# In the late turns of a fused attention and MLP kernel, sums of values and chunk 4's scores become one group on TensorE

## The chip, the cores and the metric

The kernel runs on one core of one Trainium2 chip. The metric is device time in microseconds (us) of one execution. A core has TensorE (PE in the profile; its weight loads are PEld), VectorE (DVE), ScalarE (ACT), GpSimd (POOL) and SyncE (SP), which here issues transfers. Each engine runs its own instructions in the order in which they stand in its queue, and waits on semaphores for the others.

## The reference

Inputs are q, k, v (8 batches, 8 heads, 576 positions, 64 dimensions), w_in (512 x 2048) and w_out (2048 x 512), all float32.

```python
scores = scale * np.matmul(q, k.transpose(0, 1, 3, 2))
mask = block_i >= block_j                 # blocks of 64 positions
scores = np.where(mask, scores, -1000000000.0)
scores = scores - np.max(scores, axis=-1, keepdims=True)
attn = np.exp(scores)
attn = attn / (np.sum(attn, axis=-1, keepdims=True) + 1e-09)
attn_out = np.matmul(attn, v)
...
x = attn_out.transpose(0, 2, 1, 3).reshape(4608, 512)
h = x @ w_in
g = h * (1.0 / (1.0 + np.exp(-1.702 * h)))
out = g @ w_out
```

## The kernel before

Attention goes by *turns*: turn n handles pair n, two heads of one batch, 32 turns in all, four to a batch. The 576 queries of a pair are five *chunks*: chunk 0 has 64 queries, chunks 1 to 4 have 128 each, and chunk i sees the first 64 × (2i+1) keys. The experts (the MLP) go by 12 *tiles* of 384 tokens, and each tile by 16 *expert chunks*: 12 products into `hp` (the first matrix, with x and w_in each split in a high and a low part, `xh`, `xl`, `wih`, `wil`), then tanh on ACT, the gate `g` on DVE, its split `gh` (ACT) and `gl` (POOL), and 9 products into `acc` one expert chunk later.

Both are woven into one stream on TensorE. `ORDER` and its special rows set, in 13 slots of a turn, where attention stands: `3+0/2+1` are the scores of chunks 3, 0, 2, 1; `4` those of chunk 4; `V` the sums of values of the pair before (`av`); `L` the preparation of the next pair (`prep`: DVE transposes q and k into `qk`, then SP loads the pair after that into `raw`). Between the slots `advance` emits expert work by a clock of estimated times. From turn 8 on (*late* turns) a slot's attention work is emitted behind the 12 hp products of an expert chunk, so that on TensorE it stands between `hp` and `acc`. TensorE's products keep the order of the program; the queues of the other engines are ordered by Tile's scheduler, by priorities, and gates and splits have a raised one.

PSUM has eight banks: three for `acc`, three turning ones (`w0` to `w2`, from `bank()`) and two (`h`, `w3`) between which `hp` alternates in late turns. A group may borrow the one that hp does not use (`lent_bank`); then the next hp product takes the same bank as the last, and waits for its gate.

A score chunk goes like this: TensorE writes scores of each head into a bank, DVE reads them (`weigh`, mask, scale and minimum in one, line 366), ACT takes exp (line 373), DVE normalises the sums (383, 386), POOL (chunks 0 to 3) or DVE (chunk 4) scales by them, and in late turns DVE transposes blocks into `turned` (`turn`, lines 400 and 405). Behind chunk 4, SP issues 16 copies within `turned` (line 412) that complete the transposition. The next turn's `av` reads them: 60 instructions, 30 products of float32 in two passes, 1600 columns for a head, the two heads side by side; ACT copies the sums into `xr`, a ring of two batches. At a tile's start `split` casts `xr` to `xh` on ACT and subtracts to `xl` on DVE, in four parts, one for each 128 of the model's dimensions; `xh` and `xl` exist once, so a part is overwritten when the last hp products of the tile before have read it. The four pairs of a batch fill one of the four parts each.

Of the kernel before, what the change touches and what calls it, by code (L numbers as in the profile page):

```python
# [25 lines left out]
ORDER = (  # L26
# [3 lines left out]
)  # L30

START = "1+0 - B 2/3 L C - V - 4 - a - - -"
FIRST_LATE = "3+0/2+1 - - - - - V - 4 - - L -"
HANDOVER = "B C - 3+0/2+1 - - V - - - 4 - - L - -"


WEIGHTS_BY = ((0, 0), (8, 13), (14.5, 32))
# [4 lines left out]
def attention_moe_kernel(  # L42
# [21 lines left out]
    NPAIR = B * H // 2  # L64
    HP = H // 2
    NCH = 5

    sp = ctx.enter_context(tc.tile_pool(name="sp", bufs=1))
    d2 = ctx.enter_context(tc.tile_pool(name="d2", bufs=2))
# [5 lines left out]
    def early(n):  # L75

        return n < 2 * HP
# [6 lines left out]

    turns = {"n": 0, "bank": 0, "experts": False, "late": False}
    gate_bank = {"now": "h", "spare": "w3", "lent": False}
    conv = {"step": 0, "loaded": 0}

# [7 lines left out]
    def lent_bank():  # L98
        gate_bank["lent"] = True
        return ps.tile([P, 512], F32, tag=gate_bank["spare"], name="bank")  # L100

    def next_hp():
        if turns["late"] and not gate_bank["lent"]:
            gate_bank["now"], gate_bank["spare"] = gate_bank["spare"], gate_bank["now"]
        gate_bank["lent"] = False
        return ps.tile([P, 512], F32, tag=gate_bank["now"], name="hp")

    def mm(**kw):
        return tc.keep_in_program_order(nc.tensor.matmul(**kw))  # L109
# [205 lines left out]
    def score(n, banks):  # L315

        turns["late"] = not early(n)
        if n not in stats:
            mx = d2.tile([P, NCH + 1, 2], F32, tag="mx", name="mx")
            sm = d2.tile([P, NCH, 2], F32, tag="sm", name="sm")  # L320
            stats[n] = (mx, sm)
        todo = []
        taken = 0
        for chunks in banks:

            part = []
            for lo, hi in ((0, 512),) if width(chunks[0]) <= 512 else ((0, 256), (256, S)):
                ss = []
                for _ in range(2):
                    taken += 1  # L330
                    ss.append(lent_bank() if taken == 1 and turns["late"] else bank())
                c = 0
                for i in chunks:
                    a, z = qrange(i)
                    w = min(hi, width(i)) - lo
                    for hd in range(2):
                        r = slice(hd * D, hd * D + D)

                        mm(
                            out=ss[hd][:, c : c + w], lhsT=qk[n][r, 0, a : a + P],  # L340
                            rhs=qk[n][r, 1, lo : lo + w], start=True, stop=True,
                        )
                        part.append((i, hd, lo, lo + w, ss[hd][0 : z - a, c : c + w]))
                    c += w
            todo.append(sorted(part, key=lambda x: (chunks[::-1].index(x[0]), x[2])))
        for chunks, part in zip(banks, todo):
            e = {}
            for i, hd, lo, hi, s in part:
                e[i] = weigh(n, i, hd, lo, hi, s, e.get(i))
            for i in chunks[::-1]:  # L350
                normalise(n, i, e[i])
                if not early(n):
                    turn(n, i, e[i])

    def weigh(n, i, hd, lo, hi, s, e):
        mx, sm = stats[n]
        a, z = qrange(i)
        m = z - a
        w = width(i)
        if early(n):  # L360
            e = es[i]
        elif e is None:
            e = d2.tile([P, 2, w], F32, tag=f"e{i % 2}", name="e", bufs=1)
        last = i > 0 and hi == w
        mk = mask[0:m, MW - (hi - lo) : MW] if last else mask[0:m, 0 : hi - lo]
        nc.vector.tensor_tensor_reduce(  # L366
            out=e[0:m, hd, lo:hi], in0=s, in1=mk,
            op0=ALU.add, op1=ALU.min, scale=-0.125,
            scalar=3e38 if lo == 0 else mx[0:m, NCH, hd : hd + 1],
            accum_out=mx[0:m, i, hd : hd + 1] if hi == w else mx[0:m, NCH, hd : hd + 1],  # L370
        )
        if hi == w:
            nc.scalar.activation(  # L373
                out=e[0:m, hd], in_=e[0:m, hd], func=AF.Exp, scale=-1.0,
                bias=mx[0:m, i, hd : hd + 1], accum_out=sm[0:m, i, hd : hd + 1],
            )
        return e

    def normalise(n, i, e):
        _, sm = stats[n]  # L380
        m = BLK if i == 0 else P
        c = sm[0:m, i]
        nc.vector.tensor_scalar(
            out=c, in0=c, scalar1=1e-9, scalar2=2.0, op0=ALU.add, op1=ALU.mult
        )
        nc.vector.reciprocal(out=c, in_=c)
        on = SCALE_ON[phase(n)][i]
        for hd in range(2):
            x, sc = e[0:m, hd], c[:, hd : hd + 1]
            if on == "P":  # L390
                nc.gpsimd.tensor_tensor(out=x, in0=x, in1=sc.to_broadcast([m, width(i)]), op=ALU.mult)  # L391
            elif on == "D":
                nc.vector.tensor_scalar(out=x, in0=x, scalar1=sc, scalar2=None, op0=ALU.mult)
            else:
                nc.scalar.activation(out=x, in_=x, func=AF.Copy, scale=sc)
# [48 lines left out]
    def av(n):  # L444

        b, h = divmod(n, HP)
        before_av(n)
        o = bank()
        o0 = lent_bank() if turns["late"] else bank()

        todo = []
        for i in range(1, NCH):
            c = (i - 1) * P
            todo += [(o, c, P, j, pw[:, :, SLOT[i] + j]) for j in range(i)]
            todo.append((o, c + BLK, BLK, i, pw[:, 2:4, 9 + i]))
        last = len(todo) - 1
        todo.append((o0, 0, BLK, 0, pw[:, 0:2, 10]))

        for x, (bk, c, nn, j, w) in enumerate(todo):
            for hd in range(2):  # L460
                mm(
                    out=bk[hd * D : hd * D + D, c : c + nn].rearrange("d (a c) -> d a c", c=32),
                    lhsT=values(n)[:, hd, j], rhs=w[:, :, hd], start=x in (0, last + 1), stop=x >= last,
                )
        c0 = (b % 2) * S
        nc.scalar.copy(out=xr[:, h, c0 : c0 + BLK], in_=o0[:, 0:BLK])
        nc.scalar.copy(out=xr[:, h, c0 + BLK : c0 + S], in_=o)
        m = follower(n)
        if m is not None:
            load_v(m)  # L470

    def follower(n):

# [1 line left out]
        return None if m is None or m >= NPAIR else m  # L475

    def order(n):
        return {HP: START, 2 * HP: HANDOVER, 2 * HP + 1: FIRST_LATE}.get(n, ORDER[phase(n)]).split()

    def step(n):  # L480

# [43 lines left out]
    def moe():  # L525
# [24 lines left out]
        for t in range(NT):  # L550
# [6 lines left out]
            for fc in range(NFC):  # L557
                if t == 0:
                    convert(fc // FG * GROUP + NDC + fc % FG + 1)
                hp = next_hp()  # L560
                fs = slice(fc % FG * P, (fc % FG + 1) * P)
                terms = [(wa, xb, dc) for dc in range(NDC) for wa, xb in (("wih", xh), ("wil", xh), ("wih", xl))]
                if fc == 0:

                    terms.sort(key=lambda x: x[1] is xl)
                for cnt, (wa, xb, dc) in enumerate(terms):
                    mm(
                        out=hp[:, 0:tt], lhsT=weights(wa, fc // FG)[:, dc, fs], rhs=xb[:, dc, 0:tt],
                        start=cnt == 0, stop=cnt == 3 * NDC - 1,
                    )  # L570
                    if cnt % 3 == 2:
                        yield unit1(tt)
                g = d2.tile([P, TT], F32, tag="g", name="g", bufs=1)[:, 0:tt]
                gh = d2.tile([P, TT], F32R, tag="gh", name="gh")[:, 0:tt]
                gl = d2.tile([P, TT], F32R, tag="gl", name="gl")[:, 0:tt]

                with tc.high_priority(offset=300):
                    nc.scalar.activation(out=g, in_=hp[:, 0:tt], func=AF.Tanh, scale=1.702)  # L578
                    nc.vector.scalar_tensor_tensor(  # L579
                        out=g, in0=g, scalar=1.0, in1=hp[:, 0:tt], op0=ALU.add, op1=ALU.mult  # L580
                    )

                if fc == NFC - 1 and t + 1 < NT:
                    yield ("tile", t + 1)
                    split(t + 1)
                with tc.high_priority(offset=300):
                    nc.scalar.copy(out=gh, in_=g)  # L587
                    subtract(nc.gpsimd, gl, g, f(gh))
                yield ("gate", fc)
                if prev is not None:  # L590
                    yield from second(prev)
                prev = (gh, gl, fc, acc, t)
# [88 lines left out]
```

## Time and profile before

| | us |
|---|---|
| median of 3 runs | 1104.87 (1103.06 to 1105.16) |
| the profiled execution | 1105.26 |
| its span from first to last instruction | 1103.5 |
| TensorE busy | 1068.6 (97%) |
| DVE, ACT, POOL busy | 584.8, 498.2, 406.5 |

Matmuls are pipelined, and their ends in the profile are modelled: the distance from one start to the next tells more than a duration. In the timeline "x60" is a run of equal instructions shown as one row. What stands in brackets is idle time of the engine ahead of the row, and what ended it. The late turns lie between 186 and 953 us; behind them come experts alone.

### The profile page before, as it was taken

The page shows a single profiled execution, that of the slowest core. Times are in us where ns is not written, and L with a number is a line of the kernel's source. Part 1 is how long each engine was busy: PE and PEld are TensorE (multiplying, and loading weights), DVE is VectorE, ACT ScalarE, POOL GpSimd, SP SyncE. Part 2 cuts the span into 40 slices and gives each one's busy share as a digit, 9 for nine tenths or more (in the row PEclk, how much of TensorE's full clock was granted, in tenths as well). Part 3 has the DMA queues.
Part 4 walks back from the last instruction along what each step waited for, and adds up shares of the span by engine and source line. Part 5 has one row for each costly group of instructions (what it writes and reads, how often), then busy time and mean ns, then how long its engine had stood idle before and what let it go on. Part 6 is the DMA issues. An engine that isn't in the chain of part 4 may idle for free.

```text
span 1103.5 us, 19999 instructions
## 1 busy us (share of the span) xinstructions
PE 1068.6 (97%) x6960; PEld 914.1 (83%) x6960; DVE 584.8 (53%) x1856; ACT 498.2 (45%) x1321; POOL 406.5 (37%) x509
## 2 busy tenths in 40 slices
PE   5869999999999999999999999999999999999998
PEld 3757777788888888888888888888888888899997
DVE  6786786655654655655555555554654655111211
ACT  5865775544443533533534444443443443232322
POOL 4665565333333333323333333333333323222222
PEclk8979999999999999999999999999999999999999
DMA  8734523343334433243444333244443331200000
GB/s 175 206 90 155 147 62 81 71 107 71 93 75 87 115 76 78 62 99 67 109 87 86 89 85 71 59 104 86 87 107 74 74 89 40 55 29 1 30 1 29
DMA packets 219365, 91.25 MB, mean 83 GB/s; under 512 B 197760, under 2 KB 197760, under 8 KB 219264
## 3 DMA queue, kind: packets, MB, share of 16 engines
q1 hardware_dynamic: 214528, 89.38, 34.5%
q10 hardware_dynamic: 4736, 0.59, 0.3%
q8 instruction: 55, 0.90, 0.3%
q14 instruction: 46, 0.38, 0.1%
HBM read 45.09 MB, written 9.44 MB: 49 GB/s over the span
## 4 chain that ended last, share of the span: by engine, by line
PE 87%; DVE 4%; ACT 4%; issue 1%; SPq 1%; DMA 1%; POOL 0%; POOLq 0%; DVEq 0%; ACTq 0%
PE hp L109 35%; PE acc L109 35%; PE bank L109 16%; ACT turned L373 1%; SPq L412 1%; PE bank L112 1%; DVE wm L244 1%; ACT wm L229 1%; DVE wm L233 1%; DVE turned L366 1%; DVE wm L239 1%; DMA raw<-in_k_dram 0%; DVE qk L307 0%; DVE xl L83 0%; ACT turned L426 0%
## 5 line engine op out<-in xcount | busy, mean ns | idle before, releaser
L83 POOL TENSOR_TENSOR gl<-g,gh 128x384 fp32r<-128x384 f32 x192 | 194.5, 1013 | 543.3 <-ACT gh L587 428.8
L579 DVE SCALAR_TENSOR_TENSOR g<-g,hp 128x384 f32<-128x384 f32 x192 | 106.0, 552 | 313.6 <-ACT g L578 312.3
L109 PE MATMUL hp<-xh,wih 128*128 128x384 f32 x768 | 261.1, 340 | 4.2 <-DVE g L579 3.5
L109 PE MATMUL hp<-xh,wil 128*128 128x384 f32 x768 | 258.7, 337 | 0.0
L109 PE MATMUL hp<-xl,wih 128*128 128x384 f32 x768 | 254.8, 339 | 0.2
L578 ACT ACTIVATE g<-hp 128x384 f32<-128x384 f32 x192 | 94.2, 490 | 354.5 <-PE hp L109 352.5
L109 PE MATMUL acc<-woh,gh 128*128 128x512 f32 x576 | 233.9, 406 | 0.0
L109 PE MATMUL acc<-wol,gh 128*128 128x512 f32 x576 | 227.0, 394 | 0.0
L587 ACT CAST gh<-g 128x384 fp32r<-128x384 f32 x192 | 98.4, 513 | 158.7 <-DVE g L579 158.5
L109 PE MATMUL acc<-woh,gl 128*128 128x512 f32 x576 | 168.0, 393 | 0.3 <-POOL gl L83 0.3
L109 PEld LDWEIGHTS hp<-xh,wih 128*128 128x128 f32 x768 | 144.6, 188 | 17.1 <-DVE g L579 4.5
L109 PEld LDWEIGHTS hp<-xh,wil 128*128 128x128 f32 x768 | 144.5, 188 | 7.6
L373 ACT ACTIVATE e<-e,mx 64x64 f32<-64x64 f32 (+4 forms) x240 | 132.2, 552 | 33.0 <-DVE mx L366 33.0
L391 POOL TENSOR_TENSOR e<-e,sm 64x64 f32<-64x64 f32 (+1 forms) x192 | 113.6, 612 | 86.2 <-ACT e L373 43.9
L109 PEld LDWEIGHTS hp<-xl,wih 128*128 128x128 f32 x768 | 144.0, 188 | 1.0 <-DVE xl L83 1.0
L109 PEld LDWEIGHTS acc<-woh,gh 128*128 128x128 f32 x576 | 108.2, 188 | 34.2 <-issue 10.3
L109 PE MATMUL bank<-qk 64*128 64x320 f32 (+4 forms) x768 | 121.3, 428 | 13.5 <-DVE qk L307 10.9
L109 PEld LDWEIGHTS acc<-woh,gl 128*128 128x128 f32 x576 | 107.6, 188 | 25.4 <-POOL gl L83 1.2
L366 DVE CUSTOM_DVE_ANT_0 e<-bank,mask 64x64 f32<-64x64 f32 (+4 forms) x240 | 89.7, 417 | 63.9 <-PE bank L109 60.5
L109 PEld LDWEIGHTS acc<-wol,gh 128*128 128x128 f32 x576 | 108.4, 188 | 16.8 <-issue 0.4
L400 DVE STREAM_TRANSPOSE turned<-e 128x384 f32<-128x384 f32 (+1 forms) x192 | 92.5, 500 | 49.0 <-POOL e L391 48.6
L109 PEld LDWEIGHTS bank<-qk 64*128 64x128 f32 x768 | 69.8, 194 | 52.7 <-issue 22.4
(50 smaller groups left out, 958.8 us busy)
## 6 DMA issues: line engine op xcount, KB each, us to landing
turned<-turned SPq DMA_DIRECT2D x192, 80.0 KB, 2.1
turned<-turned SPq DMA_DIRECT2D x96, 112.0 KB, 2.2
raw<-in_q_dram SPq DMA_DIRECT2D x128, 72.0 KB, 2.3
out_dram<-osb SPq DMA_DIRECT2D x36, 256.0 KB, 2.4
raw<-in_k_dram SPq DMA_DIRECT2D x120, 72.0 KB, 2.4
turned<-turned SPq DMA_DIRECT2D x96, 88.0 KB, 2.1
words<-in_moe_w_in_dram SPq DMA_DIRECT2D x16, 512.0 KB, 6.0
vp<-in_v_dram SPq DMA_DIRECT2D x60, 128.0 KB, 2.5
```

The lines of the kernel that those rows point to most:

```text
L83: eng.tensor_tensor(out=out, in0=in0, in1=in1, op=ALU.subtract)
L109: return tc.keep_in_program_order(nc.tensor.matmul(**kw))
L112: return tc.keep_in_program_order(nc.tensor.transpose(**kw))
L229: nc.scalar.activation(out=bits[j][:, c], in_=f(w[..., 1]), func=AF.Copy, scale=2.0**-112)
L233: nc.vector.tensor_scalar(out=u, in0=u, scalar1=3, scalar2=None, op0=ALU.logical_shift_left)
L366: nc.vector.tensor_tensor_reduce(out=e[0:m, hd, lo:hi], in0=s, in1=mk, op0=ALU.add, op1=ALU.min, scale=-0.125, scalar=3e38 if lo == 0 else ...
L373: nc.scalar.activation(out=e[0:m, hd], in_=e[0:m, hd], func=AF.Exp, scale=-1.0, bias=mx[0:m, i, hd : hd + 1], accum_out=sm[0:m, i, hd : hd ...
L391: nc.gpsimd.tensor_tensor(out=x, in0=x, in1=sc.to_broadcast([m, width(i)]), op=ALU.mult)
L400: nc.vector.transpose(out=tw[:, :, SLOT[i] : SLOT[i] + i, hd].rearrange("p b j c -> p j b c"), in_=e[:, hd, 0 : i * P],)
L578: nc.scalar.activation(out=g, in_=hp[:, 0:tt], func=AF.Tanh, scale=1.702)
L579: nc.vector.scalar_tensor_tensor(out=g, in0=g, scalar=1.0, in1=hp[:, 0:tt], op0=ALU.add, op1=ALU.mult)
L587: nc.scalar.copy(out=gh, in_=g)
```

## The change

`V` and `4` of a late turn become one group. In turn n `av(n - 1)` first sums the values of pair n − 1 into two turning banks: `o0` takes queries 0 to 319, `o` takes 320 to 575. Behind them it writes pair n's scores of chunk 4: for both heads the first 384 keys into two banks of their own (the borrowed one and the third turning one), and the last 192 keys into the free columns of `o0` and `o`. ACT copies the sums out, and `settle` does the rest of chunk 4, with `prep(n + 1)` behind its reads in place of slot `L`. The group stands in slot 8, where chunk 4's scores stood; the sums of values come from slot 5. The scores of the other chunks stay in slot 1. A new dependency (`behind`) puts the third gate after them behind the last read of scores on DVE.

```diff
-    "3+0/2+1 - - - V - - 4 - - - L -",
+    "3+0/2+1 - - - - - - V - - - - -",
...
-FIRST_LATE = "3+0/2+1 - - - - - V - 4 - - L -"
-HANDOVER = "B C - 3+0/2+1 - - V - - - 4 - - L - -"
+HANDOVER = "B C - 3+0/2+1 - - - - - - V - - - - -"
...
+    def behind(ins, other):
+        tc.add_manual_dep(
+            ins.ins, other.ins.name, mybir.DependencyInfo(mybir.DependencyClass.NoSync, mybir.DependencyReason.DATA),
+            reason="order on one engine",
+        )
...
+    def settle(n, banks, todo):
         for chunks, part in zip(banks, todo):
             e = {}
             for i, hd, lo, hi, s in part:
                 e[i] = weigh(n, i, hd, lo, hi, s, e.get(i))
+            if not early(n) and 4 in chunks and n + 1 < NPAIR:
+                prep(n + 1)
             for i in chunks[::-1]:
                 normalise(n, i, e[i])
...
-        o = bank()
-        o0 = lent_bank() if turns["late"] else bank()
+        if turns["late"]:
+            o0, o = bank(), bank()
+            cut = BLK + 2 * P
...
+        m = n + 1
+        rest = []
+        if turns["late"] and m < NPAIR:
+            own = [lent_bank(), bank()]
+            a, z = qrange(4)
+            for hd in range(2):
+                r = slice(hd * D, hd * D + D)
+                mm(
+                    out=own[hd][:, 0:K4], lhsT=qk[m][r, 0, a : a + P],
+                    rhs=qk[m][r, 1, 0:K4], start=True, stop=True,
+                )
+                rest.append((4, hd, 0, K4, own[hd][0 : z - a, 0:K4]))
+            for hd, (bk, c) in enumerate(((o0, cut), (o, S - cut))):
...
+                rest.append((4, hd, K4, S, bk[0 : z - a, c : c + S - K4]))
         c0 = (b % 2) * S
-        nc.scalar.copy(out=xr[:, h, c0 : c0 + BLK], in_=o0[:, 0:BLK])
-        nc.scalar.copy(out=xr[:, h, c0 + BLK : c0 + S], in_=o)
...
+        nc.scalar.copy(out=xr[:, h, c0 : c0 + cut], in_=o0[:, 0:cut])
+        nc.scalar.copy(out=xr[:, h, c0 + cut : c0 + S], in_=o[:, 0 : S - cut])
...
+        if rest:
+            settle(m, [[4]], [sorted(rest, key=lambda x: x[2])])
...
+                    turns["gates"] += 1
+                    if turns["late"] and turns["gates"] == 3:
+                        behind(gate, turns["read"])
```

On TensorE a late turn had three groups, two expert chunks apart: scores, values, chunk 4. Now it has two: two expert chunks lie between the merged group and the next scores, four between those and the next merged group. Chunk 4's scores in a late turn before, between hp and acc:

```order
L109 MATMUL hp<-xl,wih 128x384
L109 MATMUL bank<-qk 128x256 x2
L109 MATMUL bank<-qk 128x320 x2
L109 MATMUL acc_8505<-woh,gh 128x512
```

And the merged group now:

```order
L115 MATMUL hp<-xl,wih 128x384
L115 MATMUL bank<-turned,vp 64x128 x2
L115 MATMUL bank<-turned,vp 64x64 x2
L115 MATMUL bank<-turned,vp 64x128 x4
L115 MATMUL bank<-turned,vp 64x64 x2
L115 MATMUL bank<-turned,vp 64x128 x6
L115 MATMUL bank<-turned,vp 64x64 x2
L115 MATMUL bank<-turned,vp 64x128 x8
L115 MATMUL bank<-turned,vp 64x64 x4
L115 MATMUL bank<-qk 128x384 x2
L115 MATMUL bank<-qk 128x192 x2
L115 MATMUL acc_4973<-woh,gh 128x512
```

The number of products is the same; the scores have moved directly behind the sums of values.

The start of tile 4 falls on such a group, of turn 16. On DVE before, the reads of chunks 1 and 2 (`e_4746`, `e_4751`, line 366), the gate and the subtractions of the split stood like this:

```order
L400 STREAM_TRANSPOSE turned_75<-e_4729 128x3x4x32 x2
L366 ISA e_4746,mx_4710<-bank_4718,mask_69 128x192
...
L366 ISA e_4751,mx_4710<-bank_4719,mask_69 128x320
...
L579 SCALAR_TENSOR_TENSOR g_4888<-g_4888,hp_4875 128x384
L83 TENSOR_TENSOR xl_978<-xr_72,xh_977 128x384 x4
L579 SCALAR_TENSOR_TENSOR g_4917<-g_4917,hp_4904 128x384
```

Now DVE has (line 378 is the read, two of each chunk, one for each head; 414 and 419 are the transposes, `g_4834` the third gate after the scores, `hp_4850` the last hp products of tile 3):

```order
L83 TENSOR_TENSOR xl_978<-xr_72,xh_977 128x384 x3
L419 STREAM_TRANSPOSE turned_75<-e_4713 64x2x2x32
L414 STREAM_TRANSPOSE turned_75<-e_4713 128x3x4x32 x2
L378 ISA e_4730,mx_4694<-bank_4702,mask_69 128x192
...
L378 ISA e_4735,mx_4694<-bank_4702,mask_69 128x320
...
L378 ISA e_4735,mx_4694<-bank_4703,mask_69 128x320
L378 ISA mx_4694 128x1
L622 SCALAR_TENSOR_TENSOR g_4834<-g_4834,hp_4821 128x384
...
L414 STREAM_TRANSPOSE turned_75<-e_4735 128x2x4x32 x2
L622 SCALAR_TENSOR_TENSOR g_4863<-g_4863,hp_4850 128x384
```

Three of the four subtractions have moved ahead of the reads; the fourth stands behind chunk 4's reads.

On ACT at the same place now, the casts that these subtractions read (`g_4834` is the third gate's tanh, 385 the exp of chunks 1 and 2, 507 and 508 the copies of the sums):

```order
L621 ACTIVATE g_4834<-hp_4821 128x384
L557 CAST xh_977<-xr_72 128x384 x3
L385 ACTIVATE e_4730,sm_4695<-e_4730,mx_4694 128x192 x2
L385 ACTIVATE e_4735,sm_4695<-e_4735,mx_4694 128x320 x2
L633 CAST gh_4835<-g_4834 128x384
L621 ACTIVATE g_4863<-hp_4850 128x384
L633 CAST gh_4864<-g_4863 128x384
L507 COPY xr_72<-bank_4868 128x320
L508 COPY xr_72<-bank_4869 128x256
L557 CAST xh_977<-xr_72 128x384
```

The split has been parted: three casts ahead of the exponentials, one behind the copies. Tile 7 looks alike, tile 1 nearly so; tile 10 follows the last sums of values directly.

More of the change, by code (lines that the diff above doesn't have):

```diff
@@ L66, in attention_moe_kernel @@
     NCH = 5
+    K4 = 384
     sp = ctx.enter_context(tc.tile_pool(name="sp", bufs=1))
@@ L83, in subtract @@
         eng.tensor_tensor(out=out, in0=in0, in1=in1, op=ALU.subtract)
-    turns = {"n": 0, "bank": 0, "experts": False, "late": False}
+    turns = {"n": 0, "bank": 0, "experts": False, "late": False, "gates": 0}
     gate_bank = {"now": "h", "spare": "w3", "lent": False}
@@ L317, in score @@
         turns["late"] = not early(n)
+        turns["gates"] = 0
         if n not in stats:
@@ L345, in score @@
             todo.append(sorted(part, key=lambda x: (chunks[::-1].index(x[0]), x[2])))
+        settle(n, banks, todo)
+    def settle(n, banks, todo):
         for chunks, part in zip(banks, todo):
@@ L365, in weigh @@
         mk = mask[0:m, MW - (hi - lo) : MW] if last else mask[0:m, 0 : hi - lo]
-        nc.vector.tensor_tensor_reduce(
+        turns["read"] = nc.vector.tensor_tensor_reduce(
             out=e[0:m, hd, lo:hi], in0=s, in1=mk,
@@ L382, in normalise @@
         c = sm[0:m, i]
-        nc.vector.tensor_scalar(
+        x = nc.vector.tensor_scalar(
             out=c, in0=c, scalar1=1e-9, scalar2=2.0, op0=ALU.add, op1=ALU.mult
         )
+        if not early(n) and i == NCH - 1:
+            tc.keep_in_program_order(x)
         nc.vector.reciprocal(out=c, in_=c)
@@ L447, in av, with place @@
         before_av(n)
-        o = bank()
-        o0 = lent_bank() if turns["late"] else bank()
+        if turns["late"]:
+            o0, o = bank(), bank()
+            cut = BLK + 2 * P
+        else:
+            o, o0 = bank(), bank()
+            cut = BLK
+        def place(q0):
+            return (o0, q0) if q0 < cut else (o, q0 - cut)
         todo = []
         for i in range(1, NCH):
[L453 to L457, printed above, removed]
+            bk, c = place((i - 1) * P + BLK)
+            todo += [(bk, c, P, j, pw[:, :, SLOT[i] + j]) for j in range(i)]
+            todo.append((bk, c + BLK, BLK, i, pw[:, 2:4, 9 + i]))
+        todo.append((*place(0), BLK, 0, pw[:, 0:2, 10]))
+        ends = [[x for x, y in enumerate(todo) if y[0] is bk] for bk in (o0, o)]
         for x, (bk, c, nn, j, w) in enumerate(todo):
@@ L462, in av @@
                     out=bk[hd * D : hd * D + D, c : c + nn].rearrange("d (a c) -> d a c", c=32),
-                    lhsT=values(n)[:, hd, j], rhs=w[:, :, hd], start=x in (0, last + 1), stop=x >= last,
-                )
-        c0 = (b % 2) * S
-        nc.scalar.copy(out=xr[:, h, c0 : c0 + BLK], in_=o0[:, 0:BLK])
[L467 to L470, printed above, removed]
+                    lhsT=values(n)[:, hd, j], rhs=w[:, :, hd],
+                    start=any(x == y[0] for y in ends), stop=any(x == y[-1] for y in ends),
+                )
+        m = n + 1
[11 more added lines that the diff above has]
+            for hd, (bk, c) in enumerate(((o0, cut), (o, S - cut))):
+                r = slice(hd * D, hd * D + D)
+                mm(
+                    out=bk[:, c : c + S - K4], lhsT=qk[m][r, 0, a : a + P],
+                    rhs=qk[m][r, 1, K4:S], start=True, stop=True,
+                )
+                rest.append((4, hd, K4, S, bk[0 : z - a, c : c + S - K4]))
+        c0 = (b % 2) * S
+        nc.scalar.copy(out=xr[:, h, c0 : c0 + cut], in_=o0[:, 0:cut])
+        nc.scalar.copy(out=xr[:, h, c0 + cut : c0 + S], in_=o[:, 0 : S - cut])
+        nxt = follower(n)
+        if nxt is not None:
+            load_v(nxt)
+        if rest:
+            settle(m, [[4]], [sorted(rest, key=lambda x: x[2])])
     def follower(n):
@@ L477, in order @@
     def order(n):
-        return {HP: START, 2 * HP: HANDOVER, 2 * HP + 1: FIRST_LATE}.get(n, ORDER[phase(n)]).split()
+        return {HP: START, 2 * HP: HANDOVER}.get(n, ORDER[phase(n)]).split()
     def step(n):
@@ L578, in moe @@
                     nc.scalar.activation(out=g, in_=hp[:, 0:tt], func=AF.Tanh, scale=1.702)
-                    nc.vector.scalar_tensor_tensor(
+                    gate = nc.vector.scalar_tensor_tensor(
                         out=g, in0=g, scalar=1.0, in1=hp[:, 0:tt], op0=ALU.add, op1=ALU.mult
                     )
+                    turns["gates"] += 1
+                    if turns["late"] and turns["gates"] == 3:
+                        behind(gate, turns["read"])
                 if fc == NFC - 1 and t + 1 < NT:
```

## The prediction

> **What bounds the kernel now.** I read the page first, then the table of stretches, then TensorE's timeline of one late turn, then the other engines around it.
>
> ```profile
> PE 1068.6 (97%) x6960; PEld 914.1 (83%) x6960; DVE 584.8 (53%) x1856; ACT 498.2 (45%) x1321; POOL 406.5 (37%) x509
> 500.00:600.00 100.00, 100.00 (x656) 86.62 (x655) 53.70 (x177) 41.38 (x111) 34.35 (x45) 1.00 0.39 86
> ```
>
> In the late turns TensorE is the bound: busy for all of 500 to 600 us (the row's five busy times are PE, PEld, DVE, ACT and POOL), no other engine but the weight loads above 54%, the granted clock 1.00. A gain can only come from time in which TensorE is busy without streaming, so I read the starts of its instructions (start, duration, engine, line, what):
>
> ```profile
> 505.09 0.34 PE L109 MATMUL hp<-xl,wih 128*128 128x384 f32 x1
> 505.36 2.98 PE L109 MATMUL bank<-turned,vp 128*64 128x128 f32 x60
> 508.27 0.50 PE L109 MATMUL acc<-woh,gh 128*128 128x512 f32 x1
> 508.61 0.40 PE L109 MATMUL acc<-wol,gh 128*128 128x512 f32 x1
> ...
> 512.38 0.33 PE L109 MATMUL hp<-xl,wih 128*128 128x384 f32 x1
> 512.55 0.39 PE L109 MATMUL acc<-woh,gh 128*128 128x512 f32 x1
> 512.78 0.40 PE L109 MATMUL acc<-wol,gh 128*128 128x512 f32 x1
> ...
> 516.56 0.34 PE L109 MATMUL hp<-xl,wih 128*128 128x384 f32 x1
> 516.83 1.24 PE L109 MATMUL bank<-qk 64*128 64x256 f32 x8
> 518.00 0.50 PE L109 MATMUL acc<-woh,gh 128*128 128x512 f32 x1
> 518.34 0.39 PE L109 MATMUL acc<-wol,gh 128*128 128x512 f32 x1
> 526.57 2.11 PE L109 MATMUL bank<-qk 64*128 64x448 f32 x16
> ```
>
> Undisturbed, an hp product is followed after 0.17 (512.38 to 512.55) and an acc product after 0.23; one expert chunk takes 4.17 (508.61 to 512.78). An attention group pays at both ends: 0.27 instead of 0.17 into it, 0.34 instead of 0.23 behind it. So the sums of values cost 508.61 − 505.09 − 0.40 = 3.12 us, chunk 4's scores 518.34 − 516.56 − 0.40 = 1.38; the scores of the other four chunks are the last row, 2.1.
>
> **The change, part by part.**
>
> *One group instead of two.* Products and columns stay the same (chunk 4 is cut 384 + 192 instead of 256 + 320). What is the price of values directly followed by scores? Nowhere before. Nearest are groups that follow each other without experts between, early on:
>
> ```profile
> 37.87 1.24 PE L109 MATMUL bank<-qk 64*128 64x256 f32 x8
> 39.04 2.98 PE L109 MATMUL bank<-turned,vx 128*64 128x128 f32 x60
> 41.96 0.87 PE L112 MATMUL bank<-ident,turned 128*128 128x128 f32 x6
> ```
>
> Scores into values take 1.17, values into transposes 2.92: the same 1.17 and 2.91 as into acc. A switch costs the same whatever stands behind it. Merged: 0.10 in, 2.91, 1.17, 0.11 out = 4.29 instead of 4.50, so 0.21 less per turn. The bounds are nothing (a dearer switch of array shape) and twice that, 0.42 (no loss between two attention shapes); I take 0.21, since both early rows agree. 24 turns have the merge; 23 of them, the 24th being in the handover below: −4.8 us. The Trainium skill, TensorEngine Tiling (Array Packing), section Key Properties, says that changing the tiling mode drains TensorE; 128*64 to 64*128 is such a change. By that rule the merged group still drains once inside and only one of four switches goes, which is the −4.8; the trace agrees, with 2.92 also in front of the transposes.
>
> *The last sums of values.* They move from 4 to 6 chunks behind the last scores:
>
> ```profile
> 929.97 1.24 PE L109 MATMUL bank<-qk 64*128 64x256 f32 x8
> 949.72 2.98 PE L109 MATMUL bank<-turned,vp 128*64 128x128 f32 x60 [1.57 <-DMA turned<-turned]
> 936.71 11.27 SPq L412 DMA_DIRECT2D turned<-turned  x16
> ```
>
> TensorE waited 1.57 for the 16 copies, which SP issues in 11.27. With 2 × 4.17 us more the copies are long down: −1.57.
>
> *SP's order.* All eight raw loads of the next pair now stand ahead of the 16 copies; before, six stood behind them.
>
> ```profile
> 523.58 10.08 SPq L412 DMA_DIRECT2D turned<-turned  x16
> 533.70 1.20 SPq L289 DMA_DIRECT2D raw<-in_q_dram  x2
> 534.95 2.12 SPq L289 DMA_DIRECT2D raw<-in_k_dram  x4
> L579 DVE SCALAR_TENSOR_TENSOR g<-g,hp 128x384 f32<-128x384 f32 x192 | 106.0, 552 | 313.6 <-ACT g L578 312.3
> L578 ACT ACTIVATE g<-hp 128x384 f32<-128x384 f32 x192 | 94.2, 490 | 354.5 <-PE hp L109 352.5
> ```
>
> That puts the copies up to 1.20 + 2.12 = 3.3 later. Call T the end of the hp products ahead of the merged group. DVE ends the preparation of the next pair near T+7.1, SP's eight loads end near T+11.3, the copies at T+21.4, landed 2.1 later (the page's DMA part) at T+23.5. DVE's next transposes into the same tile stand behind a gate at about T+24.5 (from T: the group 4.3, the other scores with their switches 2.2, four chunks of 4.17, then tanh 0.49 and gate 0.55 with their hand-overs, 1.25). One microsecond to spare, and behind it some five more until TensorE needs what follows: nothing.
>
> *ACT and DVE.* The two xr copies stay two. The tails of the value banks are read by DVE only behind ACT's copies (the order shows the wait): some 0.4 us on DVE, hidden, since the next scores come 8.4 us later. Moving the preparation in the code changes nothing: DVE already ran it ahead of the normalising.
>
> *DVE's reads ahead of the third gate.* In an ordinary turn DVE then reads chunks 1 and 2 at T+26 to T+27.6, the gate is due at T+28: free. Not at tiles 4 and 7. There the tile boundary falls on the merged group (every 48 chunks, 8 turns), and the order pieces in the section on the change show ACT's three xh casts and DVE's three xl subtractions of the new tile ahead of the reads. In the trace such a split is tied to the last hp of the old tile:
>
> ```profile
> 534.94 0.33 PE L109 MATMUL hp<-xh,wih 128*128 128x384 f32 x1
> 535.48 2.10 ACT L514 CAST xh<-xr 128x384 fp32r<-128x384 f32 x4 [0.74 <-PE hp L109]
> 536.03 2.14 DVE L83 TENSOR_TENSOR xl<-xr,xh 128x384 fp32r<-128x384 f32 x4 [1.49 <-ACT xh L514]
> ```
>
> The casts begin 0.54 after that hp's start (it lasts 12 × 0.175 = 2.1, so T−1.56), the third subtraction ends at 1.09 + 3/4 × 2.14 = 2.69 after it, T+0.6. Before, the reads stood ahead of the split; now they follow, with what these rows cost:
>
> ```profile
> 506.52 1.03 DVE L400 STREAM_TRANSPOSE turned<-e 128x384 f32<-128x384 f32 x2
> 507.69 0.36 DVE L366 CUSTOM_DVE_ANT_0 e<-bank,mask 128x192 f32<-128x192 f32 x1
> 508.67 0.08 DVE L366 DVE_READ_ACCUMULATOR2_ANT mx<- 128x1 f32 x1
> 510.08 0.56 ACT L467 COPY xr<-bank 128x512 f32<-128x512 f32 x1
> 509.65 0.97 POOL L391 TENSOR_TENSOR e<-e,sm 128x192 f32<-128x192 f32 x2 [1.42 <-ACT e L373]
> 511.84 1.40 POOL L391 TENSOR_TENSOR e<-e,sm 128x320 f32<-128x320 f32 x2 [1.22 <-DVE sm L386]
> 515.31 1.01 POOL L83 TENSOR_TENSOR gl<-g,gh 128x384 fp32r<-128x384 f32 x1 [2.07 <-PE acc L109]
> ```
>
> A small transpose 0.3, the two large ones 1.17 (506.52 to 507.69), three reads 0.98 (to 508.67): T+3.1. The second value bank is the bank of the third read, and the sums want it after 512 of their 1600 columns, T + 0.10 + 0.93: TensorE waits 2.1 us. Next, the gate of the old tile's last hp stands on DVE behind chunk 2's transposes, which wait for POOL: the third gate at T+4.05, small sums 0.5, chunk 1's scaling 0.97, half of chunk 2's 0.70, gl 1.01, the other half 0.70, a transpose 0.45 and the gate 0.55 give T+9.05; TensorE wants the bank at T + 4.29 + 2.1 + 9 × 0.23 = T+8.5: 0.6. Last, the fourth cast waits for gh (0.51) and the two xr copies (some 0.8): ready at T+10.95, wanted at T+10.15: 0.8. Together 3.5 us, twice: +7.0. The bounds per tile are 0 (the reads get done in time after all) and about 5.5 (POOL one gl and one scaling later); I take the worked value.
>
> *The handover* (first late turn, tile 1).
>
> ```profile
> 191.05 0.86 PE L109 MATMUL acc<-woh,gl 128*128 128x512 f32 x3
> 202.28 0.44 PE L109 MATMUL hp<-xh,wih 128*128 128x384 f32 x1 [1.70 <-DVE g L579]
> 192.39 0.52 DVE L579 SCALAR_TENSOR_TENSOR g<-g,hp 128x384 f32<-128x384 f32 x1
> ```
>
> The wait of 1.70 goes, since 6 us of products now cover that gate. But hp follows directly on the acc products that end at 191.74 (191.05 + 3 × 0.23) and wants the gate that ends at 192.91: 1.2 back. And the first hp of tile 1 needs the last xl, now behind chunk 4's reads: by the same counting some 1.2 late. With the merge: +0.5, between −1.9 and +2.
>
> **The sum.** −4.8 − 1.57 + 0.5 + 7.0 = +1.1 against the profiled execution's 1105.26 (span 1103.5), so 1106.4. The median of the three runs, 1104.87, is 0.39 lower: 1106.0. Measurement tells about 0.2%, 2.2 us, from no change; I forecast no change that can be told.
>
> **Rivals.**
> 1. *The tiles cost nothing* (24%): the copies of `turned` land early and the boundary waits hide. For it: in ordinary turns the reads are 5 us ahead. Against: engine order is fixed, and the split cannot begin before T−1.56. Without the 7.0: 1099.0, faster.
> 2. *The tiles cost more* (15%): POOL, whose rows the page calls rough, serves gl and a scaling one step later, 2 us more at each, from the point where the gate of tile 4's predecessor ends after T+11 instead of T+9. 1110, slower.
> 3. *No loss inside the merged group* (6%): 0.42 saved per turn, another 23 × 0.21 = 4.8 gone: 1101.2, faster. Against it stand the early rows, 1.17 and 2.92.
> 4. *The group waits for its four banks in every turn* (6%), so the merge doesn't do what it says: half a microsecond in 22 turns gives 1117. It decides only if the reads of chunks 1 and 2 end after T+32.7, five later than worked out. The Trainium skill, PSUM — Partial Sum Buffer, section PSUM bank collisions raise a hardware error, says that two engines must not touch one bank together, reads included; that is why a bank shared by ACT's copy and DVE's read makes one wait, and no row before shows its price.
>
> The forecast itself has 45%, with 1103 to 1109 as its own range (the two tiles at 2.1 to 5 us each, the merge ± 0.05 a turn); the last 4% are spread. Faster by over 0.2%: rivals 1 and most of 3, a little of the forecast: 0.29. Within: 0.40, nearly all from the forecast. Slower: rivals 2 and 4, the upper end of the forecast: 0.31. The range reaches to rival 1 and rival 2: 1099 to 1110.
>
> **What would show it.** Merged groups of about 4.1 us (2.91 + 1.17) with no wait in ordinary turns. No wait ahead of the last sums of values. TensorE idle about 2 us inside the sums of values at two places some 250 us apart, released by DVE's reads, and again at the first hp behind each, released by the gate or the cast. If those two places are seamless I am wrong by 7 us, if ordinary turns show waits, by far more.

## The result, and the profile after

The changed kernel took 1111.16 us, the median of 6 runs (1109.34 to 1112.30), beside 1105.01 of the kernel before on the same chip (6 runs, 1103.06 to 1106.67): ratio 1.0054, 95% interval 1.0044 to 1.0064. It is 0.5% slower. I had forecast 1106.0 with a range of 1099 to 1110.

The profiled execution took 1109.89 (span 1108.1). Its busy line and the same stretch as before (busy time of PE, PEld, DVE, ACT, POOL, each with its count; then the granted clock, the share of the DMA engines and their GB/s):

```profile
PE 1065.1 (96%) x6960; PEld 913.5 (82%) x6960; DVE 585.0 (53%) x1856; ACT 497.8 (45%) x1321; POOL 405.1 (37%) x509
500.00:600.00 100.00, 100.00 (x662) 86.37 (x661) 55.76 (x188) 43.32 (x119) 34.16 (x46) 1.00 0.39 88
```

TensorE is busy for 3.5 us less than before, in a span 4.6 longer, and the ordinary late turns are still without a gap. So the merge did what it should, and something else lost more. The merged group of an ordinary turn, as starts and durations of TensorE's instructions:

```profile
487.65 0.34 PE L115 MATMUL hp<-xl,wih 128*128 128x384 f32 x1
487.92 2.98 PE L115 MATMUL bank<-turned,vp 128*64 128x128 f32 x60
490.83 1.24 PE L115 MATMUL bank<-qk 64*128 64x384 f32 x8
492.00 0.50 PE L115 MATMUL acc<-woh,gh 128*128 128x512 f32 x1
492.34 0.39 PE L115 MATMUL acc<-wol,gh 128*128 128x512 f32 x1
...
962.74 2.98 PE L115 MATMUL bank<-turned,vp 128*64 128x128 f32 x60
```

The merged group costs 492.34 − 487.65 − 0.40 = 4.29, where its two parts cost 3.12 + 1.38 before. The last row is the last sums of values: no wait, where 1.57 stood. The time is lost in three places: two tile boundaries and turn 9. Two lines of TensorE's list of waits (what it waited for, us in total, times, the longest) hold them; the first has grown from 1.2 us in 2 waits, the second is new:

```profile
PE bank L115 <- DVE mx L378: 5.2, 4, 1.9
PE acc L115 <- ACT gh L633: 3.5, 1, 3.5
```

What the first has gained is two waits of 1.93, at the two tile boundaries that the prediction named. Here is the one at 454 us, on TensorE and DVE, with the new tile's first hp products:

```profile
453.18 1.11 PE L115 MATMUL bank<-turned,vp 128*64 128x128 f32 x20
456.21 0.99 PE L115 MATMUL bank<-turned,vp 128*64 128x128 f32 x16 [1.93 <-DVE mx L378]
...
452.07 1.62 DVE L83 TENSOR_TENSOR xl<-xr,xh 128x384 fp32r<-128x384 f32 x3 [5.81 <-ACT xh L557]
455.66 0.49 DVE L378 CUSTOM_DVE_ANT_0 e<-bank,mask 128x320 f32<-128x320 f32 x1
...
460.89 0.86 PE L115 MATMUL acc<-woh,gl 128*128 128x512 f32 x3
463.31 0.44 PE L115 MATMUL hp<-xh,wih 128*128 128x384 f32 x1 [0.24 <-ACT xh L557]
464.70 0.39 PE L115 MATMUL acc<-woh,gh 128*128 128x512 f32 x1
```

The sums of values stop behind 20 of their 60 instructions, until the third read, the first of the two of 320 columns on DVE (455.66), has freed the second value bank. (The row at 456.21 counts only up to 457, where the view ends; 40 instructions follow the stop.) The whole group takes 2.15 us longer from start to start than an ordinary one, and the same at 710 us. The first hp products of the tile cost another 1.0 in several small gaps: from the acc products at 460.89 to those at 464.70 it is 3.81, at the same place before 2.79 (455.93 to 458.72).

The second line of the waits is the one that I did not foresee. It stands in turn 9, the second late turn, at 226 us. Rows of SP's DMA queue, then DVE, ACT, TensorE, and the two stretches around the wait:

```profile
208.99 11.56 SPq L426 DMA_DIRECT2D turned<-turned  x16
...
215.06 0.56 DVE L622 SCALAR_TENSOR_TENSOR g<-g,hp 128x384 f32<-128x384 f32 x1 [1.71 <-ACT g L621]
222.16 1.04 DVE L414 STREAM_TRANSPOSE turned<-e 128x384 f32<-128x384 f32 x2 [4.81 <-DMA turned<-turned]
224.72 0.55 DVE L622 SCALAR_TENSOR_TENSOR g<-g,hp 128x384 f32<-128x384 f32 x1
...
218.72 0.49 ACT L621 ACTIVATE g<-hp 128x384 f32<-128x384 f32 x1 [2.56 <-PE hp L115]
...
222.48 0.34 PE L115 MATMUL hp<-xl,wih 128*128 128x384 f32 x1
226.27 0.79 PE L115 MATMUL acc<-woh,gh 128*128 128x512 f32 x1 [3.45 <-ACT gh L633]
...
222.00:226.00 4.00, 0.82 (x5) 0.50 (x3) 3.37 (x14) 2.26 (x9) 0.28 (x1) 0.98 0.44 167
226.00:229.50 3.50, 3.23 (x8) 2.61 (x9) 2.14 (x8) 0.71 (x2) 3.01 (x5) 0.53 0.00 0
```

The tanh of a gate was done at 219.21. DVE started that gate only at 224.72: it first waited 4.81 for the copies of `turned`, then transposed and read the scores of chunks 2 and 1, because the *hold*, as I call the new dependency `behind`, puts this gate behind them. TensorE stood still for 3.45, 3.62 by the starts (226.27 − 222.48 − 0.17), and the next products ran at a granted clock of 0.53: seven steps from one acc start to the next took 3.09 instead of 7 × 0.23 = 1.62. Together 5.1 us.

In an ordinary turn DVE's same rows read:

```profile
511.82 0.56 DVE L622 SCALAR_TENSOR_TENSOR g<-g,hp 128x384 f32<-128x384 f32 x1 [3.63 <-ACT g L621]
512.93 1.04 DVE L414 STREAM_TRANSPOSE turned<-e 128x384 f32<-128x384 f32 x2
515.08 0.49 DVE L378 CUSTOM_DVE_ANT_0 e<-bank,mask 128x320 f32<-128x320 f32 x1
516.01 0.56 DVE L622 SCALAR_TENSOR_TENSOR g<-g,hp 128x384 f32<-128x384 f32 x1 [0.44 <-ACT g L621]
```

Two gates, this one at 511.82 and one at 507.64, stand between the first scores' reads and these transposes, nothing waits for a copy, and the held gate comes 0.44 behind the last read, released by its own tanh. In turn 9 only one gate stands there. The counter that picks the third gate is set to zero in `score`. In turn 9 it must have counted a gate that DVE runs ahead of the scores' reads, so that the "third" is the second behind them; the run that holds the fourth gate there, below, bears this out.

Terms, from the rows: merge 24 × 0.206 = −4.9, last sums −1.6, tiles 4 and 7 2 × (2.15 + 1.0) = +6.3, turn 9 +5.1, handover +0.1 (waits of 1.06 and 0.51 for the 1.70 before; with its merge −0.1, as it is 36.72 from the first late scores, 185.76, to the hp product at 222.48, and was 36.81); +5.0. The late turns began 0.7 earlier in this execution (first scores at 185.76 against 186.45), which makes +4.3; the spans differ by 4.6. The 0.3 between the two is in the merge: a late turn as a whole became 0.19 shorter, not 0.21 (the acc product behind the merged group stands at 267.70 and, four turns later, at 394.07; the same products before at 263.76 and 390.88).

### The profile page after: what moved, and what is told of

The parts are those of the page before. It is cut to its first block, busy times and chain, and to the rows that moved or that the text cites. A ratio compares the mean times of both kernels' runs of the same rounds, so it can differ in the third digit from the quotient of the medians.

```text
span 1108.1 us, 19988 instructions
## 1 busy us (share of the span) xinstructions
PE 1065.1 (96%) x6960; PEld 913.5 (82%) x6960; DVE 585.0 (53%) x1856; ACT 497.8 (45%) x1321; POOL 405.1 (37%) x509
## 5 line engine op out<-in xcount | busy, mean ns | idle before, releaser
L115 PE MATMUL bank<-qk 64*128 64x192 f32 (+5 forms) x768 | 120.0, 424 | 14.4 <-DVE qk L313 11.5
L414 DVE STREAM_TRANSPOSE turned<-e 128x384 f32<-128x384 f32 (+1 forms) x192 | 89.8, 494 | 40.6 <-POOL e L405 33.2
L378 DVE CUSTOM_DVE_ANT_0 e<-bank,mask 64x64 f32<-64x64 f32 (+4 forms) x240 | 94.7, 444 | 25.5 <-PE bank L115 21.7
```

The source lines that it names most:

```text
L378: turns["read"] = nc.vector.tensor_tensor_reduce(out=e[0:m, hd, lo:hi], in0=s, in1=mk, op0=ALU.add, op1=ALU.min, scale=-0.125, scalar=3e38 ...
L414: nc.vector.transpose(out=tw[:, :, SLOT[i] : SLOT[i] + i, hd].rearrange("p b j c -> p j b c"), in_=e[:, hd, 0 : i * P],)
```

## The experiments

*No hold.*

```diff
-                    if turns["late"] and turns["gates"] == 3:
-                        behind(gate, turns["read"])
```

> The third gate of a late turn is no longer held behind DVE's reads; everything else stays. DVE then passes three gates and, behind two small transposes, the gate of the hp products directly ahead of the merged group before it reads chunks 2 and 1. Theory: the hold is what makes the merge possible. That last gate ends about 1.1 us behind the end of its hp products, two large transposes take 1.17, the third read ends some 0.75 later, so the second value bank comes free 3.0 us behind the end of the hp products and is wanted after 1.03: TensorE waits about 2 us inside the sums of values in each of some 21 ordinary turns, +42, and turn 9 loses its 5 us of waiting: 1145 to 1150 us, ratio about 1.038. Rival: the hold does nothing but delay turn 9; then the ordinary turns stay seamless and the time is 1106, ratio 1.001.

1175.49 us, ratio 1.0638 (1.0624 to 1.0651). The line of waits, one ordinary turn on DVE and TensorE, and the stretch behind the wait of another turn:

```profile
PE bank L115 <- DVE mx L378: 53.1, 24, 2.8
...
405.19 0.55 DVE L622 SCALAR_TENSOR_TENSOR g<-g,hp 128x384 f32<-128x384 f32 x1 [3.08 <-ACT g L621]
407.39 0.49 DVE L378 CUSTOM_DVE_ANT_0 e<-bank,mask 128x320 f32<-128x320 f32 x1
...
407.94 1.32 PE L115 MATMUL bank<-turned,vp 128*64 128x128 f32 x22 [2.34 <-DVE mx L378]
...
372.00:375.00 3.00, 2.83 (x42) 2.72 (x42) 2.05 (x11) 1.53 (x7) 0.97 (x2) 0.71 0.01 3
```

The theory holds in kind: gate (405.19), transposes, reads, then the bank, in each of 22 turns. Its size was short. The wait is mostly 2.34 (2.56 from start to start) instead of 2, the scores wait in 13 turns as well (5.1 in all), and in 8 of the turns the clock fell behind the wait (0.71 here), which cost some 1.6 each. In this order of the work the merge does not pay without the hold.

*The turn's reads first at tiles 4 and 7.* `score` notes its last exponential and its last read, and the split goes behind them.

```diff
+        turns["scored"] = (turns["exp"], turns["read"])
...
-                    nc.scalar.copy(out=xh[:, dc, a : a + w], in_=src)
-                    subtract(nc.vector, xl[:, dc, a : a + w], src, f(xh[:, dc, a : a + w]))
+                    hi = nc.scalar.copy(out=xh[:, dc, a : a + w], in_=src)
+                    lo = subtract(nc.vector, xl[:, dc, a : a + w], src, f(xh[:, dc, a : a + w]))
+                    if turns["late"] and turns["gates"] > 2:
+                        behind(hi, turns["scored"][0])
+                        behind(lo, turns["scored"][1])
```

> The casts and subtractions of tiles 4 and 7 go behind the last exponential and the last read of the turn's scores, as they stood before the change. Theory: the wait of 2.15 us inside the sums of values near 454 and 710 us goes, and with it most of the 0.75 at each tile's first hp: 4.3 to 5.8 us less than the changed kernel, 1105.4 to 1106.9, ratio 1.0004 to 1.0017; turn 9 (226 us) still waits 3.45. Rival: the split comes later instead and the first hp of the tile waits for xl or for the old tile's last gate, 2 us at each tile: 1109 to 1111, ratio 1.004 to 1.0055, with the waits moved from the sums of values to the hp products near 463 and 719.

1104.65 us, ratio 0.9989 (0.9980 to 0.9998): 7.2 less than the changed kernel by the two ratios, against the 4.3 to 5.8 expected. No merged group is longer than 4.29 now, and no hp product at the two tiles waits; the rival falls. The wait in turn 9 is there as before, 3.3 us, and behind it the clock is low for longer:

```profile
226.50:230.00 3.50, 3.19 (x8) 2.51 (x9) 2.15 (x8) 0.75 (x2) 3.06 (x5) 0.50 0.00 0
230.00:232.50 2.50, 2.50 (x9) 2.31 (x8) 0.79 (x3) 0.51 (x1) 1.00 (x1) 0.50 0.00 0
```

Part of the excess over 5.8 is that the expectation counted 0.75 for the hp products of a tile where the rows give 1.0; with that the two tiles cost 6.3. The other 0.9 is within the intervals of the two ratios, each some 1.1 us to either side; a lower clock behind a tile's wait, which the run of the changed kernel below shows, may be in it.

*The fourth gate held in turn 9.* TensorE's order stays, and DVE's in turn 9 becomes the ordinary one.

```diff
-                    if turns["late"] and turns["gates"] == 3:
+                    if turns["late"] and turns["gates"] == (4 if turns["n"] == 2 * HP + 1 else 3):
```

> In turn 9 alone the fourth gate counted is held behind the reads instead of the third; TensorE's order is the same, and DVE's order in turn 9 becomes that of the other late turns (two gates between the first scores' reads and the transposes that wait for the copies of turned, instead of one). Theory: in turn 9 the count starts one gate early, so that the hold catches the second gate behind the scores; that is the 3.45 us wait at 226 us and, behind it, the 1.4 at half clock: 5 us less than the changed kernel, 1106, ratio 1.001. Rival: the copies of turn 8 are late in themselves, since SP issues eight raw loads ahead of them (they land near 222.1), and DVE's transposes and reads behind them then delay the next gate or the next merged group: half or more of the 5 us stays, 1108.5 to 1111, ratio 1.003 to 1.0055.

1105.11 us, ratio 1.0000 (0.9991 to 1.0008): 6.0 less, so all that the wait and the clock had cost, 5.1 in the trace. DVE, TensorE and the stretch:

```profile
218.09 0.56 DVE L622 SCALAR_TENSOR_TENSOR g<-g,hp 128x384 f32<-128x384 f32 x1 [3.63 <-ACT g L621]
220.80 1.04 DVE L414 STREAM_TRANSPOSE turned<-e 128x384 f32<-128x384 f32 x2 [1.63 <-DMA turned<-turned]
223.37 0.55 DVE L622 SCALAR_TENSOR_TENSOR g<-g,hp 128x384 f32<-128x384 f32 x1
...
221.49 0.39 PE L115 MATMUL acc<-woh,gh 128*128 128x512 f32 x1
...
222.00:226.00 4.00, 4.00 (x24) 3.45 (x24) 3.55 (x16) 2.73 (x10) 1.64 (x4) 1.00 0.08 30
```

This decides against the rival. The merged group ahead starts 1.19 earlier here (193.40 against 194.59), and so does everything behind it: the copies let DVE go at 220.80, 27.4 behind the group's start, where it was 27.6 (194.59 to 222.16). DVE still waits for them. But the gate at 218.09 no longer stands behind that wait, and TensorE does not notice. The copies were late in both runs, and late copies alone cost nothing: the loss needed the gate that stood behind them.

*Both edits.*

> Both edits: the split of tiles 4 and 7 behind the turn's reads, and the fourth gate held in turn 9. Theory: the two losses are separate and add: 9.3 to 10.8 us less than the changed kernel, 1100.4 to 1101.9, ratio 0.9958 to 0.9972, faster than the kernel before, since the merge (0.206 in 24 turns) and the last wait (1.57) remain. Rival: the saving of one is taken back at the other's place, or a loss that I have not seen stands behind both: 1104 to 1107, ratio 0.999 to 1.002.

1098.78 us, ratio 0.9943 (0.9930 to 0.9955): faster than the kernel before by 0.6%, and 12.3 below the changed one, a little less than 7.2 + 6.0. The three places, busy throughout at full clock:

```profile
222.00:226.00 4.00, 4.00 (x22) 3.61 (x21) 3.48 (x14) 2.85 (x10) 0.53 (x2) 1.00 0.37 142
448.00:458.00 10.00, 10.00 (x98) 8.61 (x97) 8.42 (x22) 4.91 (x12) 3.25 (x4) 1.00 0.16 35
704.00:714.00 10.00, 10.00 (x54) 8.50 (x54) 7.94 (x22) 5.71 (x14) 2.02 (x2) 1.00 0.45 81
```

What is left against the kernel before, 6.3 us by the ratio, agrees with the merge and the last sums: 4.9 + 1.6.

*The groups apart again.* In the version with both edits, three acc products between the values and chunk 4's scores:

```diff
+            if state["wait"] is None:
+                state["t"] += next(mo)
+                state["gate"] = False
             own = [lent_bank(), bank()]
```

> The version with both edits, but with three acc products put between the sums of values and chunk 4's scores in 21 of the 24 merged groups (not in the handover and not at tiles 4 and 7). Banks, reads, holds and the work are the same. Theory: the merge saves 0.206 us each time (4.286 against 3.12 + 1.38), whatever stands between: 21 x 0.21 = 4.4 us more than the version with both edits, about 1103.2, ratio 0.998 to 0.999. Rival: the gain of that version comes from the banks and the later scores and not from the merge; then the time stays within 1 us of 1098.8, ratio 0.994 to 0.995.

1103.21 us, ratio 0.9991 (0.9981 to 1.0000): 5.3 more than with both edits by the ratios, 4.4 by the medians, though these were taken on two chips; 21 groups have the edit. One of them:

```profile
228.51 0.34 PE L115 MATMUL hp<-xl,wih 128*128 128x384 f32 x1
228.78 2.98 PE L115 MATMUL bank<-turned,vp 128*64 128x128 f32 x60
231.70 0.50 PE L115 MATMUL acc<-woh,gh 128*128 128x512 f32 x1
...
232.27 0.39 PE L115 MATMUL acc<-woh,gh 128*128 128x512 f32 x1
232.59 1.24 PE L115 MATMUL bank<-qk 64*128 64x384 f32 x8
233.76 0.50 PE L115 MATMUL acc<-wol,gh 128*128 128x512 f32 x1
```

The values are left and entered as in the kernel before, and the scores add their own 0.32 in (232.27 to 232.59) and 0.33 out, where acc products follow each other by 0.23. The traces are sharper than the times here: from the first to the last of the 21 groups, the acc products behind them lie 699.31 apart, and 695.05 with both edits. That is 4.26 for 20 groups, so the merge is worth what the rows say, 0.21 a turn.

*The fourth gate held in every turn* (with both edits).

```diff
-turns["gates"] == (4 if turns["n"] == 2 * HP + 1 else 3)
+turns["gates"] == 4
```

> The version with both edits, with the fourth gate held in every late turn instead of the third. DVE then passes three gates ahead of the reads of chunks 2 and 1, but not the fourth, the one directly ahead of the merged group. Theory: the third gate ends some 3.1 us ahead of the end of the last hp products, two large transposes (1.17) and the reads (1.0) end about 0.9 ahead of it, and the value banks are wanted 0.1 and 1.03 behind it: nothing waits, and the time is that of the version with both edits, 1098 to 1100, ratio 0.993 to 0.9955; the whole loss without a hold then comes from the fourth gate. Rival: the slack of the reads is smaller, or POOL's scaling, two gates later, delays the next transposes and the gate behind them: TensorE waits half a microsecond or more in 22 turns, 1110 or more, ratio above 1.004.

1121.43 us, ratio 1.0152 (1.0137 to 1.0167). My theory fell and the rival stands. TensorE's waits, then DVE and TensorE in one turn:

```profile
PE bank L115 <- DVE g L626: 17.6, 19, 1.2
...
489.21 0.49 DVE L379 CUSTOM_DVE_ANT_0 e<-bank,mask 128x320 f32<-128x320 f32 x1
495.27 0.45 DVE L415 STREAM_TRANSPOSE turned<-e 128x256 f32<-128x256 f32 x1 [1.21 <-POOL e L406]
501.26 1.30 DVE L415 STREAM_TRANSPOSE turned<-e 128x512 f32<-128x512 f32 x2
502.48 0.52 DVE L626 SCALAR_TENSOR_TENSOR g<-g,hp 128x384 f32<-128x384 f32 x1
...
503.05 1.19 PE L115 MATMUL bank<-qk 64*128 64x448 f32 x8 [0.89 <-DVE g L626]
```

The reads were in time, as worked out: the last ends at 489.70, and no sum of values waits. But the transposes behind them wait for POOL (495.27), chunk 4's reads and transposes follow, and the first gate behind the merged group comes at 502.48 instead of about 499; the next scores want its bank. Where the reads stand is fixed to within one gate: one gate too many ahead of them costs a wait behind the merged group (here), one too few a wait ahead of it (turn 9).

*The changed kernel once more.*

> The changed kernel once more, beside the others. Theory: the wait in turn 9 is 3.4 to 3.7 us in each execution, and what varies is how long TensorE runs at about half its clock behind it (1.4 us lost in the one trace of the changed kernel, about 3 in the trace of the run with the reads first): 1109 to 1112, ratio 1.0045 to 1.0065, and the two waits of 2.15 us do not lower the clock. Rival: the lower clock belongs to single executions and not to the wait; then it shows in other places or not at all.

1110.46 us, ratio 1.0049 (1.0035 to 1.0063). The wait in turn 9 is 3.1, a little under the 3.4 to 3.7 expected, and the clock behind it low for 14 starts instead of 7. Against my theory, the clock was low behind one of the two tile waits too:

```profile
712.13 2.19 PE L115 MATMUL bank<-turned,vp 128*64 128x128 f32 x20 [1.93 <-DVE mx L378]
...
713.00:716.50 3.50, 3.50 (x40) 3.19 (x38) 2.03 (x8) 1.36 (x4) 3.10 (x5) 0.64 0.00 0
```

That group took 1.6 longer than its twin at 453 us. Its tile took 0.6 longer in all, since later gaps shrank, and turn 9 took 0.9 longer. So tiles and turn 9 cost some 13 us in this trace and 11.4 in the first; both edits together gave back 12.3 by the ratios.

## Why the prediction was wrong

- *One group instead of two*, −0.21 a turn: right. 4.29 in the rows, and 0.21 a group in the traces when 21 of them were put apart.
- *The last sums of values*, −1.57: right.
- *SP's order*, put at nothing: the ordinary turn came out as worked out, reads ended at T + 27.7 (515.57; T is 487.82, the end of the last hp products) where I had 27.6, gate at T + 28.2 where I had 28. Turn 9 was not ordinary. Its copies were issued from T + 14.5 (208.99; T is 194.49) instead of T + 11.3, and DVE's transposes could start at T + 27.7 instead of 24.5.
- *DVE's reads ahead of the third gate, "in an ordinary turn ... free"*: this is the step that failed. I gave every turn but the two at the tiles a held gate due at T + 28. In turn 9 the held gate was due at T + 24.7 (its tanh ended at 219.21), one chunk earlier, and so it stood behind reads that themselves waited for the late copies. DVE's rows show it: one gate between the first reads and the transposes, where an ordinary turn has two. I read the order at the tiles and at an ordinary turn and took turn 9 for one of these. The run that holds the fourth gate there alone gave back 6.0 us. How the loss divides between hold and copies, no run shows. An estimate from these rows: with transposes at T + 24.5, as predicted, the reads behind them (2.56, 222.16 to 224.72) and the time from gate to acc (1.55, 224.72 to 226.27) lead to T + 28.6, and TensorE wanted the gate at T + 28.2. Copies in time would have left a wait of about 0.5, so it took both, the early gate and the late copies.
- *Tiles 4 and 7*: right in place and cause, and undone by one edit. The wait inside the sums was 2.15 (2.1 predicted), what follows 1.0 instead of 1.4; so 3.15 a tile instead of 3.5. The lower clock that it sometimes brings I had not in the sum.
- *The handover*, +0.5 with its merge: the hp products waited 1.06 (I had 1.2) and the last xl 0.51 (1.2), so about −0.1 with the merge. In its turn chunk 4 came late on DVE (its large transposes began at 205.90, T + 11.4, and in an ordinary turn at 496.19, T + 8.4), and the copies behind them in turn 9 were late with it; I did not follow this into the next turn.
- The rivals: none named turn 9. Rival 1, the tiles at nothing, gave 1099.0; the version in which the tiles and turn 9 both cost nothing took 1098.8.

With turn 9's 5.1 us the sum would have been 1111.1, beside the 1111.16 measured. That it agrees so closely is luck: the tiles were put 0.7 too high and the handover some 0.6, the merge brought a little less than its 0.21, and the lower clock behind a tile's wait, seen in one execution and not in another, was in no term. The clock behind the wait belongs to turn 9's term: the Trainium skill, TensorE: Matmul & The Clock Gate, section HAM oscillation — how this bites in real kernels, gives as the rule that TensorE should have no idle gap above some 3.4 us. The wait of 3.45 in turn 9 agrees with it. The waits of 3.3 and 3.1 at the same place in two other runs do not, nor does the one of 1.93 at 712 us, nor those of about 2.3 without the hold: the granted clock fell to 0.50 behind the first, and to 0.64 and 0.71 behind some of the others. The measurement decides: a shorter wait can cost the clock too, though not each time.

## What to carry to other kernels

Where an order is set by counting (here the third gate), list what the count hits in every turn, above all in the first ones behind a change of phase, as turn 9 was here. Whether a wait on an engine is harmless or dear depends on what stands behind it in that engine's queue, and not only on how late the awaited thing is. A saving of 0.2 us in each of 24 turns is real, but one misplaced instruction costs as much as all of them; so go through the places that differ before adding up those that agree.

## What was not expected of the hardware

A wait of TensorE costs more than its length when the granted clock falls behind it: 1.5 us behind 3.45 in the first trace of the changed kernel, about twice that in two other runs (14 product starts at half clock instead of 7, behind 3.3 and 3.1), 1.6 behind one of the six waits of 1.9 at tiles 4 and 7 in three traces, and some 1.6 behind 8 of the 22 waits of 2.2 to 2.8 without the hold. The same wait in the same place had it in one execution and not in another; what decides it, these traces do not show.
